# Row sums of four heads in one matmul set, and key and query loads of 64 rows

## The chip, the cores and the metric

The kernel runs on one core of one Trainium2 chip. The metric is the time on the device in microseconds (us). TensorE (PE) does the matmuls, VectorE (DVE) and ScalarE (ACT) the elementwise work, GpSimd (POOL) and SyncE (SP) here mainly issue transfers, which 16 DMA engines carry out.

## The reference, cut to what matters

All is float32, with 2048 tokens, model width 1024 and 32 heads. The change lies in `_A_ref`.

```python
def _A_ref(x, wqkv, wo):                       # S = 2048, D = 1024, H = 32, Dh = 32
    qkv = (x @ wqkv).reshape(B, S, 3, H, Dh).transpose(2, 0, 3, 1, 4)
    q, k, v = qkv[0], qkv[1], qkv[2]
    scores = jnp.einsum("bhqd,bhkd->bhqk", q, k) * (Dh ** -0.5)
    p = _softmax(scores, axis=-1)
    o = jnp.einsum("bhqk,bhkd->bhqd", p, v)
    return o.transpose(0, 2, 1, 3).reshape(B, S, D) @ wo
...
g = _sigmoid((x * gate_w).sum(-1, keepdims=True))
return g * _A_ref(x, A_wqkv, A_wo) + (1 - g) * _B_ref(x, ...)   # B: a router over 64 experts
```

## The kernel before

The program has three stages: projections, router and values; the attention; and the output product with `wo`. In the first, q and k are each split into a high and a low part of lower precision, and `evac` stores the four in DRAM, one array [1024, 2048] for each (`QKD`). Head h owns rows 32h to 32h+31 of each.

The attention works head by head, with a step for every tile of 128 keys: 16 steps a head, 512 in all, done in twos. For two tiles, `scores` puts eight matmuls (four chunks of 512 queries each) into a ring of seven PSUM banks (tile `ring`), and ACT takes the exponentials out of it into P tiles of [128 keys x 2048 queries]. Then PE multiplies the P tiles of the two steps before with the values (`pv`, tile `o`). The key operand holds three blocks of 32 rows (high, high, low) and the query operand three (high, low, high), so that one matmul sums three products; two more rows hold a shift. `load_kq` loads both for head h+1 at step 2 of head h, with six transfers of 32 rows of 8 KB on SP's queue. Even heads use the tiles called z, odd heads K and Q.

The softmax needs for every query the sum of P over all keys. Tile 1 of a head is written into a tile `accd` of its own, and tiles 3, 8 and 12 are added to it by accumulating transfers that POOL issues (`presum`, L1385). DVE adds the other twelve into `ACC[h]`, [128 x 2048] (first L1390, then L1392). `merge`, at step 5 of the next head, adds accd to it (L1395). What is left is a sum over 128 partitions.

Heads 0 to 27 do that in pairs, during the two heads that follow. `fold_even` adds the upper 64 partitions of the even head's ACC to its lower 64 with an accumulating transfer (POOL, L1398). `copy_odd` copies the upper half of the odd head's ACC into the freed upper half of the even one (SP), and `fold_odd` adds the odd one's lower half to that (POOL, L1404). `pair_sums` multiplies with a 0/1 selection matrix `sel` in four matmuls, one for each chunk of queries (L1376, with the tile name prm for the weights), two heads at once; ACT copies the result out of the ring (L1411), and SP stores it. Heads 28 to 30 take their sums one by one with `head_sums`. ACC of heads 4g+2 lies in a tile rb0; the other even heads use acc0, the odd ones acc1.

There are eight P buffers besides accd. A buffer is written again eight tiles later (tile 1 not counted), once PE, DVE or the transfer that reads it is done. The order of each engine's instructions and of each queue is the order in which the program is written: a table `todo` gives for each step what is done after `pv`, and a queue issues strictly in that order. A transfer whose operands are not ready holds up all that come behind it on the same queue.

Of the kernel before, what the change touches and what calls it, by code (L numbers as in the profile page):

```python
# [9 lines left out]
F32 = mybir.dt.float32  # L10
F32R = mybir.dt.float32r
I32 = mybir.dt.int32
AF = mybir.ActivationFunctionType
OP = mybir.AluOpType
AX = mybir.AxisListType

S = 2048
D = 1024
# [3 lines left out]
NT = S // 128  # L22
NQ = S // 512
# [8 lines left out]
def gated_mha_peer_kernel(ctx, tc, xT, wqkv, wv, wo, wq, k12, ug, v, out):  # L32
# [8 lines left out]
    nc = tc.nc  # L41
# [4 lines left out]
    dram = ctx.enter_context(tc.tile_pool(name="dram", bufs=1, space=bass.MemoryType.DRAM))  # L46


    QKD = [[dram.tile([D, S], F32R, name=f"{n}d{part}") for part in "hl"] for n in "qk"]
    SHD = dram.tile([H, 2, S], F32R, name="shd")  # L50
    VD = [dram.tile([S, 512], F32, name=f"vd{i}") for i in range(2)]
    WPD = dram.tile([128, KC, 512], F32, name="wpd")
# [4 lines left out]
    SMD = [dram.tile([4, S], F32, name=f"smd{g}") for g in range(G)]  # L57
# [17 lines left out]
    def dma(dst, src, queue=nc.sync):  # L75
        a, b = (ap.bitcast(F32) if ap.dtype == F32R else ap for ap in (dst, src))
        return queue.dma_start(a, b)
# [16 lines left out]
    def split(hi, lo, src, on=None):  # L94
        nc.scalar.activation(hi, src, AF.Copy)
        (on or nc.vector).tensor_tensor(out=lo, in0=src, in1=hi.bitcast(F32), op=OP.subtract)
# [38 lines left out]
    def hi_of(parts, src):  # L135
        nc.scalar.activation(parts[0], src, AF.Copy)  # L136

    def lo_of(parts, src):
        nc.vector.tensor_tensor(out=parts[1], in0=src, in1=parts[0].bitcast(F32), op=OP.subtract)
# [98 lines left out]
    late = []  # L238

    def run_late():  # L240

        for f, *a in late:
            f(*a)
        late.clear()
# [11 lines left out]
    def evac(which, c, n, src, ps, hold=False):  # L256
        hi, lo = (ev.tile([128, 512], F32R, name=part) for part in ("hi", "lo"))
        hi_of((hi, lo), src)
        run_late()
        if hold:  # L260
            held.append(((hi, lo), src))
        else:
            lo_of((hi, lo), src)
        late.append((squares, ps, src, which, c, n))
        for dst, t in zip(QKD[which], (hi, lo)):
            late.append((dma, dst[128 * c:128 * c + 128, n * 512:(n + 1) * 512], t, nc.gpsimd))

    def load_kq(h, tiles):
        K, Q = tiles
        rows = slice(32 * h, 32 * h + 32)  # L270
        (qh, ql), (kh, kl) = (tuple(t[rows, :] for t in parts) for parts in QKD)
        for tile_, srcs in ((K, (kh, kh, kl)), (Q, (qh, ql, qh))):
            for i, src in enumerate(srcs):
                dma(tile_[32 * i:32 * i + 32, :], src)

    def load_shift(h, tiles):
        dma(tiles[1][96:98, :], SHD[h])
# [532 lines left out]
    def exact_maxima():  # L810
        limit_bits = int(np.float32(SHIFT_LIMIT / SCALE).view(np.int32))
        creg = nc.values_load(cbits.bitcast(I32), min_val=0, max_val=2 ** 31 - 1,
                              skip_runtime_bounds_check_because="a float's bits without its sign")

        banks = [(bank_no[0] + k) % 8 for k in range(7)]

        def bank():
            banks.append(banks.pop(0))
            return ps1.tile([128, 512], F32, name=f"bk{banks[-1]}")

        with tc.If(creg > limit_bits):
            with ExitStack() as st:
                gp = st.enter_context(tc.tile_pool(name="gp", bufs=1))
                with tc.For_i(0, H, 1) as h:
                    kt = gp.tile([96, S], F32R, name="gk")
                    hs, rows = bass.ds(h, 1), bass.ds(h * 32, 32)
                    for i, part in enumerate((0, 0, 1)):
                        dma(kt[32 * i:32 * i + 32, :], QKD[1][part][rows, :])
                    mx = gp.tile([128, NT, 4], F32, name="mx")
                    for t in range(NT):  # L830
                        if t % 8 == 0:
                            qt = gp.tile([96, S // 2], F32R, name="gq")
                            c = slice(t * 128, (t + 8) * 128)
                            for i, part in enumerate((0, 1, 0)):
                                dma(qt[32 * i:32 * i + 32, :], QKD[0][part][rows, c])
                        for n in range(4):
                            ps = bank()
                            nc.tensor.matmul(ps, qt[:, t % 8 * 128:(t % 8 + 1) * 128], kt[:, n * 512:(n + 1) * 512],
                                             start=True, stop=True)
                            nc.vector.tensor_reduce(mx[:, t, n:n + 1], ps, axis=AX.X, op=OP.max)  # L840
                    mr = gp.tile([128, NT], F32, name="mr")
                    nc.vector.tensor_reduce(mr, mx, axis=AX.X, op=OP.max, negate=True)
                    pt = bank()
                    nc.tensor.transpose(pt[:NT, :128], mr, ident)
                    hi = gp.tile([NT, 128], F32R, name="ghi")
                    lo = gp.tile([NT, 128], F32R, name="glo")
                    split(hi, lo, pt[:NT, :128])
                    for r, src in ((0, hi), (1, lo)):
                        dma(SHD[hs, r:r + 1, :].rearrange("a b (t s) -> (a b t) s", t=NT), src)
# [413 lines left out]
    keep = Pool("keep")  # L1263
# [3 lines left out]
    NP = H - 4  # L1267
    ACC = {}

    def new_acc(h):  # L1270
        if h < NP and h % 4 == 2:
            ACC[h] = keep.tile([128, S], F32, name="rb0")
        else:
            ACC[h] = wk.tile([128, S], F32, name=f"acc{h % 2}", bufs=1)

    def raw_wo(kc):
        i, j = divmod((kc - 1) % KC, 2)
# [2 lines left out]
    wk = Pool("wk", bufs=2)  # L1280

    new_acc(0)
    sel = prf
    nc.vector.memset(sel, 0.0)
    for i in range(2):
        nc.vector.memset(sel[64 * i:64 * i + 64, i:i + 1], 1.0)
    vpool = Pool("vpool", bufs=2)
    kq = Pool("kq")
    pools["left"] = Pool("ppl")
# [7 lines left out]
    ring = pss.tile([128, NB, 512], F32, name="ring")  # L1297
# [3 lines left out]
    def ring_banks(n):  # L1301
        i = [(ring_no[0] + k) % NB for k in range(n)]
        ring_no[0] += n
        return i

    def on_ring(ins, *banks):

        for other, theirs in users:
            if ins.ins.engine != other.ins.engine and not theirs & set(banks):
                tc.declare_no_dep(ins.ins, other.ins, reason="different banks of the ring")  # L1310
        users.append((ins, set(banks)))
        del users[:-6 * NB]
# [60 lines left out]
    def rowsum(ps, *srcs, by=ones):  # L1373
        for src in srcs:
            for qc in range(NQ):
                yield nc.tensor.matmul(ps[32 * qc:32 * qc + 32, :], by,  # L1376
                                       src[:, qc * 512:(qc + 1) * 512],
                                       start=(src is srcs[0]), stop=(src is srcs[-1]))
# [15 lines left out]
    def merge(h):  # L1394
        nc.vector.tensor_add(ACC[h], ACC[h], ACCD[h])  # L1395

    def fold_even(h):
        nc.gpsimd.dma_start(ACC[h][:64], ACC[h][64:], accum_op=OP.add)  # L1398

    def copy_odd(h):  # L1400
        dma(ACC[h - 1][64:], ACC[h][64:])

    def fold_odd(h):
        nc.gpsimd.dma_start(ACC[h - 1][64:], ACC.pop(h)[:64], accum_op=OP.add)  # L1404

    def pair_sums(h):
        i, = ring_banks(1)
        for ins in rowsum(ring[:, i, :], ACC.pop(h), by=sel):
            on_ring(ins, i)
        o = wk.tile([128, 512], F32, name="ssb")  # L1410
        on_ring(nc.scalar.activation(o, ring[:, i, :], AF.Copy), i)  # L1411
        g, j = divmod(h, 4)
        for m in range(2):
            dma(SMD[g][j + m:j + m + 1, :].rearrange("o (q s) -> (o q) s", q=NQ), o[m::32, :])

    def head_sums(h):
        i, = ring_banks(1)
# [72 lines left out]
    def at(step, f, *a):  # L1490
        todo.setdefault(step, []).append((f, a))

    for h in range(H):
        base = h * NT
        g, j = divmod(h, 4)
        if h < H - 1:
            at(base + NT, finish, h)
            at(base + NT + 5, merge, h)
            if h >= NP:
                at(base + NT + 8, head_sums, h)  # L1500
            elif h % 2 == 0:
                at(base + NT + 9, fold_even, h)
            else:
                at(base + NT + 8, copy_odd, h)
                at(base + NT + 10, fold_odd, h)
                at(base + 2 * NT + 2, pair_sums, h - 1)
        if j == 3 and g + 1 < G:
            at(base + 2 * NT + 8, load_r, g)
            at(base + 2 * NT + 12, norm_r, g)
        if h >= 1 and h + 1 < H:  # L1510
            at(base + 2, load_head, h + 1)
        if g + 1 < G:
            at(base + 7, load_v, g + 1, j)
    for i, step in enumerate((6, 7, 9, 11)):
        at((H - 1) * NT + step, split_first, i)
    for k in range(2 * KC):
        c = slice(k % 2 * D // 2, (k % 2 + 1) * D // 2)
# [310 lines left out]
```

## Time and profile before

| | |
|---|---|
| median of 3 runs | 1813.65 us (1811.86 to 1818.12) |
| profiled execution | 1815.41 us, of it the span 1813.6 us |
| busy: PE, DVE, ACT, POOL | 99%, 81%, 72%, 14% of the span |
| attention, first scores to last | from about 612 to 1640 us of the span |
| accumulating transfers into accd | 95 of 1 MB, median 8.5 us from issue to landing |
| folds of even heads, issued by POOL | 14 of 512 KB; median 9.3 us (acc) and 13.5 us (rb) |
| folds of odd heads into rb, issued by POOL | 7 of 512 KB, median 7.6 us |

Rows of the timeline read: start in us from the start of the span, duration in us, engine, line, operation, tile written and tiles read, count; in brackets the engine's idle time before it and what ended it. A row of busy times by stretch gives the stretch, its length, the busy time of PE, PEld, DVE, ACT and POOL, each with its number of instructions, the granted clock of TensorE, the busy share of the DMA engines and GB/s. Rows of transfers give the tile written and read, the issuing queue, the count, the size and the median time from issue to landing. q0 is the queue of POOL's transfers, q1 that of SP's. L numbers are lines of the kernel before.

### The profile page before, as it was taken

The page shows a single profiled execution, that of the slowest core. Times are in us where ns is not written, and L with a number is a line of the kernel's source. Part 1 is how long each engine was busy: PE and PEld are TensorE (multiplying, and loading weights), DVE is VectorE, ACT ScalarE, POOL GpSimd, SP SyncE. Part 2 cuts the span into 40 slices and gives each one's busy share as a digit, 9 for nine tenths or more (in the row PEclk, how much of TensorE's full clock was granted, in tenths as well). Part 3 has the DMA queues.
Part 4 walks back from the last instruction along what each step waited for, and adds up shares of the span by engine and source line. Part 5 has one row for each costly group of instructions (what it writes and reads, how often), then busy time and mean ns, then how long its engine had stood idle before and what let it go on. Part 6 is the DMA issues. An engine that isn't in the chain of part 4 may idle for free.

```text
span 1813.6 us, 26222 instructions
## 1 busy us (share of the span) xinstructions
PE 1803.4 (99%) x9959; PEld 1092.1 (60%) x9959; DVE 1473.4 (81%) x1278; ACT 1308.9 (72%) x1708; POOL 253.2 (14%) x381
## 2 busy tenths in 40 slices
PE   9999999999999999999999999999999999999999
PEld 7777777788888644444444444444444444447887
DVE  8866876789967888888898887898889888897874
ACT  6545544532343699999999999999999999994221
POOL 1222222244101100101101011100111010000000
PEclk9999999999999999999999999999999999999999
DMA  7888699560267778998899898899999889878641
GB/s 285 275 280 277 214 298 286 193 225 13 82 232 240 224 162 186 201 196 186 189 213 192 191 206 192 187 208 200 196 191 213 187 188 213 191 160 288 231 157 59
DMA packets 120210, 367.48 MB, mean 203 GB/s; under 512 B 16753, under 2 KB 49793, under 8 KB 96465
## 3 DMA queue, kind: packets, MB, share of 16 engines
q0 software_dynamic: 30192, 159.97, 39.2%
q1 hardware_dynamic: 88584, 203.57, 38.6%
q10 hardware_dynamic: 1304, 2.24, 0.3%
q8 instruction: 79, 1.29, 0.3%
q14 instruction: 51, 0.41, 0.1%
HBM read 171.99 MB, written 72.36 MB: 135 GB/s over the span
## 4 chain that ended last, share of the span: by engine, by line
PE 92%; DMA 4%; ACT 2%; issue 1%; SPq 0%; DVE 0%; ACTq 0%
PE ring L1342 25%; PE o L1363 23%; PE bk L303 15%; PE pa L973 7%; PE bk L973 6%; PE bk L734 5%; DMA accd<-P 4%; PE bk L992 2%; PE bk L291 2%; ACT P L1352 2%; PE bk L342 2%; PE pa L1573 1%; PE ring L1376 1%; PE pa L1580 1%; PE bk L191 0%
## 5 line engine op out<-in xcount | busy, mean ns | idle before, releaser
L1352 ACT ACTIVATE P<-ring 128x512 f32<-128x512 f32 (+2 forms) x1028 | 911.8, 982 | 27.5 <-DMA accd<-P 9.3
L1392 DVE TENSOR_TENSOR acc<-acc,P 128x2048 f32<-128x2048 f32 x250 | 572.9, 2291 | 67.5 <-ACT P L1352 47.8
L1363 PE MATMUL o<-P,V 128*32 128x512 f32 x3840 | 466.3, 600 | 0.0
L1342 PE MATMUL ring<-z,z 98*128 98x512 f32 x1016 | 272.3, 408 | 3.7 <-ACT P L1352 3.7
L1342 PE MATMUL ring<-Q,K 98*128 98x512 f32 x1024 | 273.2, 408 | 0.5 <-ACT P L1352 0.5
L1342 PEld LDWEIGHTS ring<-z,z 98*128 98x128 f32 x1016 | 179.9, 188 | 150.1 <-ACT P L1352 86.3
L1342 PEld LDWEIGHTS ring<-Q,K 98*128 98x128 f32 x1024 | 182.2, 188 | 146.1 <-ACT P L1352 75.7
L1363 PEld LDWEIGHTS o<-P,V 128*32 128x32 f32 x3840 | 99.1, 109 | 223.3 <-issue 215.1
L1385 POOL DMA_DIRECT2D accd<-P x95 | 82.0, 863 | 892.4 <-ACT P L1352 600.2
L1392 DVE TENSOR_TENSOR rb<-rb,P 128x2048 f32<-128x2048 f32 x70 | 160.4, 2292 | 17.4 <-ACT P L1352 11.8
L1390 DVE TENSOR_TENSOR acc<-P,P 128x2048 f32<-128x2048 f32 x25 | 57.3, 2293 | 47.5 <-ACT P L1352 47.5
L303 PE MATMUL bk<-xh,A 128*128 128x512 f32 x336 | 82.8, 396 | 0.0
L303 PE MATMUL bk<-xh,S 128*128 128x512 f32 x336 | 81.3, 393 | 0.0
L303 PE MATMUL bk<-xl,S 128*128 128x512 f32 x336 | 80.3, 391 | 0.0
L136 ACT ACTIVATE hi<-u 128x512 fp32r<-128x512 f32 x42 | 26.6, 632 | 70.1 <-issue 35.4
L303 PEld LDWEIGHTS bk<-xh,A 128*128 128x128 f32 x336 | 62.1, 188 | 23.8 <-issue 5.0
L303 PEld LDWEIGHTS bk<-xl,S 128*128 128x128 f32 x336 | 62.7, 188 | 16.6 <-issue 2.5
L303 PEld LDWEIGHTS bk<-xh,S 128*128 128x128 f32 x336 | 62.4, 188 | 14.5 <-issue 1.7
L973 PE MATMUL pa<-woh,acc 128*128 128x512 f32 x216 | 69.9, 389 | 0.0
L1352 ACT ACTIVATE accd<-ring 128x1024 f32<-128x1024 f32 (+2 forms) x65 | 62.3, 1020 | 0.1
L1395 DVE TENSOR_TENSOR acc<-acc,accd 128x2048 f32<-128x2048 f32 x25 | 57.1, 2286 | 0.3 <-DMA accd<-P 0.3
L521 DVE TENSOR_TENSOR u<-u,bk 128x512 f32<-128x512 f32 x70 | 46.6, 683 | 9.7 <-DMA wpd<-u 5.6
(326 smaller groups left out, 2254.5 us busy)
## 6 DMA issues: line engine op xcount, KB each, us to landing
accd<-P POOLq DMA_DIRECT2D x95, 1024.0 KB, 8.5
wqt<-in_wq SPq DMA_DIRECT2D x64, 512.0 KB
wraw<-in_wqkv SPq DMA_DIRECT2D x28, 512.0 KB
kdh<-hi POOLq DMA_DIRECT2D x32, 256.0 KB, 5.6
kdl<-lo POOLq DMA_DIRECT2D x32, 256.0 KB, 6.5
qdh<-hi POOLq DMA_DIRECT2D x32, 256.0 KB, 6.0
qdl<-lo POOLq DMA_DIRECT2D x32, 256.0 KB, 6.0
z<-kdh SPq DMA_DIRECT2D x32, 256.0 KB
```

The costliest lines, as they stand in the source:

```text
L291: nc.tensor.matmul(b0[w, n], AW[PLAIN[w, ki]][a][:, k, :], X[f"B{ki + 1}{n + 1}"][b][:, k, :], start=first, stop=last)
L303: nc.tensor.matmul(ps, a[i][:, k, :], b[j][:, k, :], start=(k == 0 and i == j == 0), stop=(k == HC - 1 and i == 1))
L521: nc.vector.tensor_tensor(out=out, in0=a, in1=b, op=OP.add)
L734: nc.tensor.matmul(ps, x_part(a, t // 4, kc)[:, tok], b, start=first, stop=last)
L973: nc.tensor.matmul(ps, self.a[a][i][:, k, :], self.b[b][j][k], start=(not first and k == 0 and i == j == 0), stop=(k == HC - 1 and i == 1))
L1342: on_ring(nc.tensor.matmul(ring[:, i, :], K[:98, kt * 128:(kt + 1) * 128], Q[:98, qc * 512:(qc + 1) * 512], start=True, stop=True), i)
L1352: on_ring(nc.scalar.activation(P[h, kt][:, q0 * 512:(q0 + m) * 512].rearrange("p (a m) -> p a m", a=m), ring[:, i:i + m, :], AF.Exp, scale ...
L1363: nc.tensor.matmul(O[h][32 * qc:32 * qc + 32, :], Vt[g][:, kt, 32 * j:32 * j + 32], p[:, qc * 512:(qc + 1) * 512], start=(kt == 0), stop=( ...
L1385: nc.gpsimd.dma_start(ACCD[h], P[h, kt], accum_op=OP.add)
L1390: nc.vector.tensor_add(ACC[h], P[h, 0], P[h, kt])
L1392: nc.vector.tensor_add(ACC[h], ACC[h], P[h, kt])
L1395: nc.vector.tensor_add(ACC[h], ACC[h], ACCD[h])
```

## The change

Three things are changed.

First, the high and low parts of q, and of k, lie in one DRAM array [1024, 2, 2048] each, so that for a row of q or k both parts follow each other. `load_kq` then loads the first block of an operand with one transfer of 32 rows, and the second and third together with one of 64 rows, in which high and low rows alternate. The order of the rows within the product changes alike in both operands, so the sum is the same. Four transfers replace six; the bytes are the same.

Second, every head of 0 to 27 is folded twice. `fold_half` adds the upper 64 partitions to the lower 64 (POOL). `fold_quarter(h, 0)` copies partitions 0 to 31 into a quarter of a group tile `F[g]` (SP), and `fold_quarter(h, 1)` adds partitions 32 to 63 to that quarter (POOL). F lies in rb0; ACC alternates between acc0 and acc1.

Third, `group_sums` takes the sums of four heads with one set of four matmuls, with `sel` now four columns over blocks of 32 rows, one copy by ACT and four stores by SP. Seven sets replace fourteen. A set stands at step 2 of the second head after its group's last.

```diff
-    QKD = [[dram.tile([D, S], F32R, name=f"{n}d{part}") for part in "hl"] for n in "qk"]
+    QKD = [dram.tile([D, 2, S], F32R, name=f"{n}d") for n in "qk"]
+    QK_PARTS = (1, 0), (0, 1)
...
-        for dst, t in zip(QKD[which], (hi, lo)):
-            late.append((dma, dst[128 * c:128 * c + 128, n * 512:(n + 1) * 512], t, nc.gpsimd))
+        for i, t in zip(QK_PARTS[which], (hi, lo)):
+            late.append((dma, QKD[which][128 * c:128 * c + 128, i, n * 512:(n + 1) * 512], t, nc.gpsimd))
...
-        K, Q = tiles
-        rows = slice(32 * h, 32 * h + 32)
-        (qh, ql), (kh, kl) = (tuple(t[rows, :] for t in parts) for parts in QKD)
-        for tile_, srcs in ((K, (kh, kh, kl)), (Q, (qh, ql, qh))):
-            for i, src in enumerate(srcs):
-                dma(tile_[32 * i:32 * i + 32, :], src)
+        for t, which in zip(tiles, (1, 0)):
+            src = QKD[which][32 * h:32 * h + 32]
+            dma(t[:32, :], src[:, QK_PARTS[which][0], :])
+            dma(t[32:96, :], src.rearrange("d a s -> (d a) s"))
...
-        if h < NP and h % 4 == 2:
-            ACC[h] = keep.tile([128, S], F32, name="rb0")
-        else:
-            ACC[h] = wk.tile([128, S], F32, name=f"acc{h % 2}", bufs=1)
+        ACC[h] = wk.tile([128, S], F32, name=f"acc{h % 2}", bufs=1)
...
-    for i in range(2):
-        nc.vector.memset(sel[64 * i:64 * i + 64, i:i + 1], 1.0)
+    for i in range(4):
+        nc.vector.memset(sel[32 * i:32 * i + 32, i:i + 1], 1.0)
...
-    def fold_even(h):
+    F = {}
+
+    def fold_half(h):
         nc.gpsimd.dma_start(ACC[h][:64], ACC[h][64:], accum_op=OP.add)
 
-    def copy_odd(h):
-        dma(ACC[h - 1][64:], ACC[h][64:])
-
-    def fold_odd(h):
-        nc.gpsimd.dma_start(ACC[h - 1][64:], ACC.pop(h)[:64], accum_op=OP.add)
-
-    def pair_sums(h):
+    def fold_quarter(h, i):
+        g, j = divmod(h, 4)
+        if i == 0:
+            if j == 0:
+                F[g] = keep.tile([128, S], F32, name="rb0")
+            dma(F[g][32 * j:32 * j + 32], ACC[h][:32])
+        else:
+            nc.gpsimd.dma_start(F[g][32 * j:32 * j + 32], ACC.pop(h)[32:64], accum_op=OP.add)
+
+    def group_sums(g):
         i, = ring_banks(1)
-        for ins in rowsum(ring[:, i, :], ACC.pop(h), by=sel):
+        for ins in rowsum(ring[:, i, :], F.pop(g), by=sel):
             on_ring(ins, i)
         o = wk.tile([128, 512], F32, name="ssb")
         on_ring(nc.scalar.activation(o, ring[:, i, :], AF.Copy), i)
-        g, j = divmod(h, 4)
-        for m in range(2):
-            dma(SMD[g][j + m:j + m + 1, :].rearrange("o (q s) -> (o q) s", q=NQ), o[m::32, :])
+        for j in range(4):
+            dma(SMD[g][j:j + 1, :].rearrange("o (q s) -> (o q) s", q=NQ), o[j::32, :])
...
-            elif h % 2 == 0:
-                at(base + NT + 9, fold_even, h)
             else:
-                at(base + NT + 8, copy_odd, h)
-                at(base + NT + 10, fold_odd, h)
-                at(base + 2 * NT + 2, pair_sums, h - 1)
+                at(base + NT + 9, fold_half, h)
+                at(base + NT + 10, fold_quarter, h, 0)
+                at(base + NT + 13, fold_quarter, h, 1)
+                if j == 3:
+                    at(base + 2 * NT + 2, group_sums, g)
```

Two places show how the order of the queues changes. The first is POOL's queue in heads 8 and 9, during which the sums of heads 7 and 8 are folded; accd<-P is the add of tile 3, 8 or 12. Before:

```order
L1385 DMA accd<-P_7233 128x2048
L1385 DMA accd<-P_7310 128x2048
L1404 DMA rb_6830<-acc_7046 64x2048
L1385 DMA accd<-P_7361 128x2048
L1385 DMA accd<-P_7444 128x2048
L1385 DMA accd<-P_7527 128x2048
L1398 DMA acc_7254<-acc_7254 64x2048
L1385 DMA accd<-P_7579 128x2048
```

And with the change:

```order
L1381 DMA accd<-P_7213 128x2048
L1381 DMA accd<-P_7289 128x2048
L1396 DMA acc_7026<-acc_7026 64x2048
L1381 DMA accd<-P_7341 128x2048
L1405 DMA rb_6708<-acc_7026 32x2048
L1381 DMA accd<-P_7423 128x2048
L1381 DMA accd<-P_7507 128x2048
L1396 DMA acc_7233<-acc_7233 64x2048
```

Each head has now a half fold behind the add of tile 8, and a quarter add between that of tile 12 and the next head's tile 3.

The second place is SP's queue from the loads of head 8 to the loads of head 9 (od is a head's output, smd the row sums, V values of the next group, wo_raw a piece of `wo` for the last stage). Before:

```order
L77 DMA K_5526<-kdh 32x2048 x2
L77 DMA K_5526<-kdl 32x2048
L77 DMA Q_5527<-qdh 32x2048
L77 DMA Q_5527<-qdl 32x2048
L77 DMA Q_5527<-qdh 32x2048
L77 DMA Q_5527<-shd 2x2048
L77 DMA V<-vd_67 128x4x128
L77 DMA rb_6830<-acc_7046 64x2048
L77 DMA wo_raw_5505<-in_wo 128x1x512
L77 DMA od<-osb 128x2x256
L77 DMA smd_74<-ssb 4x512 x2
L77 DMA z_4909<-kdh 32x2048 x2
```

And with the change:

```order
L78 DMA K_5524<-kd 32x2048
L78 DMA K_5524<-kd 64x2048
L78 DMA Q_5525<-qd 32x2048
L78 DMA Q_5525<-qd 64x2048
L78 DMA Q_5525<-shd 2x2048
L78 DMA V<-vd_65 128x4x128
L78 DMA rb_6708<-acc_7026 32x2048
L78 DMA wo_raw_5501<-in_wo 128x1x512
L78 DMA od<-osb 128x2x256
L78 DMA smd_72<-ssb 4x512 x4
L78 DMA z_4907<-kd 32x2048
L78 DMA z_4907<-kd 64x2048
```

The copy into rb is at the same place in the queue, but of 32 rows, and it now reads what the half fold on POOL's queue writes; such a copy stands in every head's stretch up to head 28, where before it stood in every second one.

More of the change, by code (lines that the diff above doesn't have):

```diff
@@ L827, in exact_maxima @@
                     for i, part in enumerate((0, 0, 1)):
-                        dma(kt[32 * i:32 * i + 32, :], QKD[1][part][rows, :])
+                        dma(kt[32 * i:32 * i + 32, :], QKD[1][rows, QK_PARTS[1][part], :])
                     mx = gp.tile([128, NT, 4], F32, name="mx")
@@ L834, in exact_maxima @@
                             for i, part in enumerate((0, 1, 0)):
-                                dma(qt[32 * i:32 * i + 32, :], QKD[0][part][rows, c])
+                                dma(qt[32 * i:32 * i + 32, :], QKD[0][rows, QK_PARTS[0][part], c])
                         for n in range(4):
```

## The prediction

> **What bounds the kernel now.** The page comes first: which engine is full, and what the chain of waits runs over.
>
> ```profile
> PE 1803.4 (99%) x9959; PEld 1092.1 (60%) x9959; DVE 1473.4 (81%) x1278; ACT 1308.9 (72%) x1708; POOL 253.2 (14%) x381
> PE ring L1342 25%; PE o L1363 23%; PE bk L303 15%; PE pa L973 7%; PE bk L973 6%; PE bk L734 5%; DMA accd<-P 4%; PE bk L992 2%; PE bk L291 2%; ACT P L1352 2%; PE bk L342 2%; PE pa L1573 1%; PE ring L1376 1%; PE pa L1580 1%; PE bk L191 0%
> ```
>
> TensorE carries the chain, and half of it is the attention (L1342, L1363). Two entries there belong to what changes: the row sums (L1376), and 4% in which the chain runs over a transfer that adds a P tile into accd. Next, the busy times by head of the attention, each stretch from one head's first scores to the next's: heads 8, 9, 10, 12, 14, 16, 18 and 28.
>
> ```profile
> 864.56:895.83 31.27, 31.27 (x197) 14.73 (x193) 27.16 (x13) 30.75 (x36) 3.41 (x4) 1.00 0.97 209
> 895.83:927.92 32.09, 32.09 (x205) 14.99 (x201) 27.48 (x15) 31.48 (x39) 2.55 (x3) 1.00 0.91 193
> 927.92:959.80 31.88, 31.70 (x197) 14.57 (x193) 28.37 (x14) 30.37 (x36) 4.01 (x5) 1.00 0.94 204
> 991.95:1024.11 32.16, 31.56 (x196) 14.64 (x192) 28.06 (x14) 30.54 (x36) 3.74 (x5) 1.00 0.94 200
> 1056.26:1090.92 34.66, 33.46 (x197) 14.75 (x193) 29.55 (x14) 30.86 (x37) 4.07 (x5) 0.95 0.93 197
> 1123.05:1155.58 32.53, 31.80 (x197) 14.53 (x193) 28.29 (x14) 30.55 (x37) 3.52 (x5) 1.00 0.92 198
> 1187.72:1220.03 32.31, 31.51 (x196) 14.65 (x192) 28.75 (x14) 30.78 (x37) 4.29 (x5) 1.00 0.94 202
> 1506.10:1538.01 31.91, 31.73 (x196) 14.57 (x193) 27.89 (x14) 30.48 (x37) 3.15 (x4) 1.00 0.94 214
> ```
>
> The columns are length, then PE, PEld, DVE, ACT, POOL, granted clock, DMA share, GB/s. Head 8 is the bare beat: 31.27 us, PE full, ACT 30.75 behind it, DVE with 4.1 to spare, and the DMA engines 97% busy. Head 9 has a row sum in it. The others are longer with no row sum: by 0.61, 0.89, 3.39, 1.26, 1.04 and 0.64. Of head 14's 3.39 some 1.7 (5% of 34.66, its clock being 0.95) is clock. So 6.1 us in all is another wait, shown for head 10 by the chain of waits, PE's timeline, and POOL's with the issue's landing:
>
> ```profile
> 936.90 14.16 DMA accd<-P
> 951.38 1.57 PE L1342 MATMUL ring<-z,z 98*128 98x512 f32 x5
> 953.14 0.98 PE L1342 MATMUL ring<-z,z 98*128 98x512 f32 x3 [0.18 <-ACT P L1352]
> 951.59 0.85 POOL L1385 DMA_DIRECT2D accd<-P  x1 [13.84 <-DMA accd<-P]
> accd<-P POOLq DMA_DIRECT2D x1, 1024.0 KB, 7.1
> ```
>
> Tile 3's add into accd, issued 9.0 us into the head, lands at 951.06, that is 23.1 in; its P buffer is the one that tile 11 needs, so ACT and then PE wait. Head 8 shows no wait: its add (13.0 from 873.58) lands at 22.0. The limit is about 22.3. The next add, issued 0.5 after that landing with nothing before it, takes 7.1.
>
> **The change part by part.**
>
> Row sums. PE's timeline around head 9's:
>
> ```profile
> 895.83 2.11 PE L1342 MATMUL ring<-Q,K 98*128 98x512 f32 x8
> 899.72 2.14 PE L1342 MATMUL ring<-Q,K 98*128 98x512 f32 x8
> 903.52 1.04 PE L1376 MATMUL ring<-rb,prm 128*32 128x512 f32 x8
> 904.50 2.12 PE L1342 MATMUL ring<-Q,K 98*128 98x512 f32 x8
> 908.40 2.11 PE L1342 MATMUL ring<-Q,K 98*128 98x512 f32 x8
> ```
>
> Two tiles take 3.89 or 3.90 (895.83 to 899.72, 904.50 to 908.40); with a row sum 4.78, so 0.87 or 0.88 each. Fourteen become seven: 7 x 0.87 = **-6.1 us**, all on PE. ACT loses seven copies of 0.6, which PE covered. The weights stay 128x32, so each set costs what it did.
>
> Key and query loads. Their rate with 32 rows at a time, and that of 8 KB rows into all 128 partitions (z and t3l at the tail), by the DMA view of 1000 to 1005 and of 1644 to 1648:
>
> ```profile
> DMA packets 219, 1.20 MB, mean 241 GB/s; under 512 B 72, under 2 KB 72, under 8 KB 72
> q1 hardware_dynamic: 219, 1.20, 103.1%
> DMA packets 250, 1.72 MB, mean 430 GB/s; under 512 B 35, under 2 KB 35, under 8 KB 54
> ```
>
> Six loads of 256 KB (1.57 MB) take 6.5 at 241. No row shows a 64-row load; between 241 and 430 I take 430, because it now spreads over more partitions, which is all in which the two rows differ that bears on it: 2.2 for the two small loads, 2.4 for the two large, 4.6 in all, so 1.9 sooner; the other bound is nothing. Two issues fewer on SP lie beside other work. The writes to the reordered rows carry the same pieces of 2 KB, off the path in the projections.
>
> The folds. DMA work per head, at 229 GB/s for adds (1 MB in 4.6, from the row below) and 241 for copies: before, per pair two adds and a copy of 512 KB, 6.8, so 3.4 a head; now an add of 512 KB and of 256 KB and a copy of 256 KB, 4.5. The +1.1 is less than the loads' -1.9.
>
> What it moves is the order. POOL's queue and the folds' landings, DVE's first add, and SP's queue:
>
> ```profile
> q0 software_dynamic: 112, 0.92, 111.0%
> DMA packets 112, 0.92 MB, mean 229 GB/s; under 512 B 0, under 2 KB 0, under 8 KB 0
> 915.29 0.85 POOL L1385 DMA_DIRECT2D accd<-P  x1 [9.72 <-ACT P L1352]
> 915.83 1.15 POOL L1398 DMA_DIRECT2D acc<-acc  x1
> accd<-P POOLq DMA_DIRECT2D x1, 1024.0 KB, 12.2
> acc<-acc POOLq DMA_DIRECT2D x1, 512.0 KB, 13.7
> 928.05 0.89 POOL L1385 DMA_DIRECT2D accd<-P  x1 [11.07 <-PE o L1363]
> accd<-P POOLq DMA_DIRECT2D x1, 1024.0 KB, 6.9
> 934.80 2.29 DVE L1390 TENSOR_TENSOR rb<-P,P 128x2048 f32<-128x2048 f32 x1 [1.19 <-ACT P L1352]
> 933.43 1.45 SPq L77 DMA_DIRECT2D K<-kdh  x2
> 943.00 0.52 SPq L77 DMA_DIRECT2D acc<-acc  x1
> ```
>
> Follow the last head of a group (its sum is folded during the head after it, times from that head's start), to the row sum that PE meets 7.7 into the next (903.52 less 895.83).
> - Tile 3's add lands at 22.0 in head 8. The loads ahead are 1.9 shorter; the odd copy, issued on SP 15.1 in (943.00 less 927.92) beside it, is gone, some 1.0 (half of a 2.2 us copy); the previous head's quarter add now comes before it, +1.1. So 20.2.
> - Tile 8's add: 0.5 and 7.1. The half fold behind it lands 2.0 later (929.5 against 927.5). Tile 12's add, issued 0.5 after tile 8's landing, lands 7.4 after it (6.9 more).
> - The quarter copy waits on SP for the half fold, so it reaches the engines after tile 12's add and lands 1.1 behind it. Behind it on SP stand wo_raw, after some heads rd, and the next head's od, all with time.
> - The quarter add waits on POOL for the copy: 0.5, then 1.1 of transfer and the 2.5 that an add has beside transfer (7.1 less 4.6). Behind it on POOL is only the next tile 3's add, 9.0 into the next head.
>
> Sum: 20.2 + 7.6 + 7.4 + 1.1 + 0.5 + 3.6 = 40.4, which is 9.1 into the next head: PE waits 1.4, say 1.5 with the semaphore, at seven row sums: **+10.5**. ACT has no scores left by then and waits too, and PE has no slack to make it up. Bounds: tile 8's add cannot be issued before its exp, 18.6 in (DVE's start on tile 2, 6.9, and six tiles of 1.95), against 20.7 here, so the wait is at best nothing; with the loads not faster it is 3.4.
>
> The wait in the other heads. Tile 3's landing at about 20 to 21 is inside 22.3, so **-6.1** of waits goes. DVE's first add of a head (6.9 in, 934.80) reuses the buffer that is folded during the head before, and now waits for the quarter add, which lies behind the key loads (issued from 5.5 in): 7 + 4.6 + V's 1.1 + its own 1.1, with landing, some 14 to 15. DVE has 4.1 us a head to spare, and that add's P buffer (tile 0) is next written by tile 9, from 18.6 in; the add takes 2.3, so until 16.2 nothing else waits. Cost nothing; from there on, microsecond for microsecond.
>
> Sum: -6.1 - 6.1 + 10.5 = -1.7. The profiled execution took 1815.41 (span 1813.6 and 1.8 around it), so 1813.7; it lies 1.8 above the median of 1813.65. Against the median: **1812**.
>
> **The rivals.**
>
> *No wait at the row sums.* If the quarter copy shares the engines with tile 12's add instead of queueing, it lands some 4 us sooner and F is ready. For it: between 920 and 925 both queues move at once.
>
> ```profile
> q0 software_dynamic: 113, 0.93, 88.7%
> q1 hardware_dynamic: 230, 0.26, 17.1%
> ```
>
> Against it: from 1000 to 1005 (above) only SP's queue moves, with an add issued at 1000.90 outstanding; 8 KB rows that come second wait. [...] Then -12.2: 1801.5.
>
> *Slower: the chain comes late.* If 64 rows load no faster than 32, tile 3's add lands 1.9 later: at 22 in every head, so the 6.1 stays, and the wait at the row sums is 3.4, 7 x 3.4 = 24. Sum -6.1 + 24 = +18: 1831. It decides from a wait of 1.8 on, where the gains are spent. For it: 97% busy DMA in head 8, so any delay is handed on. Against it: the 430.
>
> *Slower: DVE held by its buffer.* If the quarter add lands after 16.2, by 1 us in the 20 or so heads with the key loads ahead: +20, 1832. [...]
>
> *The row sums cost as before per head*, since weights of four columns run as long as of two: excluded, the matmul set is the same size.
>
> **How the numbers follow.** The forecast 0.44, own range 1805 to 1819 (waits of 0.5 to 2.5); no wait 0.22; late chain 0.19; held DVE 0.09; the rest, unnamed, 0.06, half each way. The range takes in the slower rivals' centres and the no-wait one: 1801 to 1831. 0.3% is 5.4 us, about what a measurement of this kernel tells from no change. Faster by more: the no-wait case, a quarter of the forecast, half the rest: 0.35. Slower: late chain and DVE, a tenth of the forecast, half the rest: 0.35 less what of the late chain stays under 5.4, so 0.32. Same: 0.33.
>
> **What would show it.** In the new profile: row-sum periods 4.78 plus the wait, seven of them; PE idle before the row sum ended by the transfer into rb; the K and Q loads done about 1.9 sooner; tile 3's add under 22 and no chain over accd at tile 11; DVE's first add some 14 in, ended by a transfer, with ACT not waiting. Wrong, if the row sums start 7.7 in without a wait, or ACT waits for P in most heads.

## The result, and the profile after

The change takes 1864.05 us (median of 4, 1859.38 to 1868.68) against 1814.93 beside it (1811.86 to 1818.12): a ratio of 1.0277, 95% interval 1.0249 to 1.0304. The forecast was 1812, with a range of 1801 to 1831. The span of the profiled execution grew from 1813.6 to 1857.5, by 43.9.

The attention accounts for all of that. Here are the busy times of the stretch from the first scores to those of the last two tiles, of the kernel before, then of the change (columns as in the prediction):

```profile
615.15:1632.04 1016.89, 1012.70 (x6233) 471.08 (x6232) 875.16 (x403) 986.21 (x1138) 105.84 (x124) 1.00 0.90 193
```

```profile
614.34:1676.21 1061.87, 1023.07 (x6178) 473.64 (x6177) 874.84 (x405) 981.55 (x1131) 129.28 (x152) 0.98 0.86 191
```

It is 45.0 us longer. TensorE's idle time in it goes from 4.2 to 38.8, which is 34.6 more; its busy time grows by 10.4, although seven row sums (7.3 us busy, by PE's groups of before) are gone. So the work that is left takes 17.7 longer, and the clock column, 0.98, points to the reason.

From the page of the change, the chain that ended last:

```profile
PE 81%; DMA 11%; DVE 3%; ACT 2%; issue 2%; POOL 0%; DVEq 0%; SPq 0%; POOLq 0%; ACTq 0%
PE ring L1338 20%; PE o L1359 18%; PE bk L302 15%; PE pa L972 7%; DMA rb<-acc 6%; PE bk L972 6%; PE bk L733 5%; PE bk L290 2%; PE bk L991 2%; DMA acc<-acc 2%; DMA accd<-P 2%; ACT P L1348 2%; DVE acc L1388 2%; PE bk L341 2%; PE pa L1573 1%
```

The chain now runs over the transfers into rb (the quarter copies and quarter adds) and over the half folds. Two engines wait for them, by the groups of PE and of DVE (busy and mean of one, then the idle time before them and what ended it):

```profile
L1372 PE MATMUL ring<-rb,prm 128*32 128x512 f32 x56 | 12.5, 975 | 28.2 <-DMA rb<-acc 14.0 <-issue 12.3 <-ACT P L1348 1.8
L1386 DVE TENSOR_TENSOR acc<-P,P 128x2048 f32<-128x2048 f32 x32 | 73.3, 2292 | 136.6 <-DMA rb<-acc 116.0 <-ACT P L1348 17.3 <-DMA V<-vd 3.3
```

And one waits for DVE, by the list of waits (total, times, longest):

```profile
ACT P L1348 <- DVE acc L1386: 15.8, 8, 4.6
```

The seven row sums stand still for 28.2 us, 4.0 each. DVE's first add of a head waits 116 us in all for the quarter add, 20 times; it has slack, but eight times the wait reaches ACT, which then cannot write tile 9's P buffer. The lateness is also handed on to the next fold, since the half fold reads what DVE's adds leave:

```profile
POOL acc L1396 <- DVE acc L1391: 9.4, 10, 1.4
```

In periods of two tiles, the distance from one pair's first scores to the next: the seven periods with a row sum and the one behind each are together 40.9 us longer than such a pair with a row sum that waits for nothing (head 9: 10.74 and 5.77 against 3.89, 3.92 and 0.87); the periods at tile 9 add 19.0 in ten heads. The waits at tile 11 (6.1, and 1.7 of clock in head 14) and seven row sums (6.1) are gone. Together +46, close to the 45.0.

Part of those periods is the clock. PE's timeline around head 9's row sum, then busy times there in pieces:

```profile
907.57 1.04 PE L1359 MATMUL o<-accd,V 128*32 128x512 f32 x8
913.50 1.93 PE L1372 MATMUL ring<-rb,prm 128*32 128x512 f32 x8 [4.89 <-DMA rb<-acc]
915.36 3.78 PE L1338 MATMUL ring<-Q,K 98*128 98x512 f32 x8
919.07 2.13 PE L1359 MATMUL o<-P,V 128*32 128x512 f32 x16
```

```profile
908.61:913.50 4.89, 0.00 (x1) 0.03 (x1) 3.50 (x3) 0.78 (x1) 1.69 (x2) 0.92 0.67 126
913.50:915.36 1.86, 1.86 (x8) 0.20 (x9) 1.86 (x1) 0.00 (x0) 0.00 (x0) 0.50 1.02 211
915.36:919.07 3.71, 3.71 (x12) 2.49 (x8) 0.92 (x2) 3.28 (x5) 0.00 (x0) 0.50 0.57 121
919.07:921.13 2.06, 2.06 (x17) 0.45 (x17) 2.06 (x2) 1.26 (x2) 0.00 (x0) 0.89 0.80 215
```

After this wait of 4.89 us TensorE runs at half clock (0.50 in the clock column), so the row sum takes 1.93 in place of 1.04 and the eight score matmuls 3.78 in place of 2.11. The change's clock records hold eight such stretches in the attention, 37.5 us in all; half of that is 18.8, close to the 17.7 of extra busy time. The kernel before had one, of 3.4 us.

Why the quarter add is late stands in the chain of waits, from head 8's start (869.33) to head 9's row sum:

```profile
876.07 2.05 ACT P L1348 x2
878.12 0.29 issue
878.41 12.55 DMA accd<-P
...
891.50 0.53 POOL accd L1381
892.03 9.49 DMA acc<-acc
...
901.58 7.35 DMA rb<-acc
...
909.48 3.78 DMA rb<-acc
913.25 0.25 issue
913.50 1.89 PE ring L1372 x5
```

Tile 3's add lands at 890.96, 21.6 into the head; the half fold, issued behind tile 8's add, lands at 901.52; the quarter copy takes 7.35 for 256 KB; only then does the quarter add start. From 878.41 to 913.25 every step is released by the landing of the one before.

### The profile page after: what moved, and what is told of

Same layout as the page of the kernel before. It is cut to its first block, busy times and chain, and to the rows that moved or that the text cites. A ratio compares the mean times of both kernels' runs of the same rounds, so it can differ in the third digit from the quotient of the medians.

```text
span 1857.5 us, 26086 instructions
## 1 busy us (share of the span) xinstructions
PE 1812.8 (98%) x9903; PEld 1095.0 (59%) x9903; DVE 1473.2 (79%) x1280; ACT 1303.8 (70%) x1701; POOL 276.6 (15%) x409
## 4 chain that ended last, share of the span: by engine, by line
PE 81%; DMA 11%; DVE 3%; ACT 2%; issue 2%; POOL 0%; DVEq 0%; SPq 0%; POOLq 0%; ACTq 0%
PE ring L1338 20%; PE o L1359 18%; PE bk L302 15%; PE pa L972 7%; DMA rb<-acc 6%; PE bk L972 6%; PE bk L733 5%; PE bk L290 2%; PE bk L991 2%; DMA acc<-acc 2%; DMA accd<-P 2%; ACT P L1348 2%; DVE acc L1388 2%; PE bk L341 2%; PE pa L1573 1%
## 5 line engine op out<-in xcount | busy, mean ns | idle before, releaser
L1348 ACT ACTIVATE P<-ring 128x1024 f32<-128x1024 f32 (+2 forms) x1028 | 910.3, 987 | 43.8 <-DVE acc L1386 15.8
L1388 DVE TENSOR_TENSOR acc<-acc,P 128x2048 f32<-128x2048 f32 x320 | 733.3, 2291 | 49.7 <-ACT P L1348 21.0
L1338 PE MATMUL ring<-Q,K 98*128 98x512 f32 x1024 | 281.7, 416 | 5.8 <-ACT P L1348 5.8
L1386 DVE TENSOR_TENSOR acc<-P,P 128x2048 f32<-128x2048 f32 x32 | 73.3, 2292 | 136.6 <-DMA rb<-acc 116.0
L1391 DVE TENSOR_TENSOR acc<-acc,accd 128x2048 f32<-128x2048 f32 x32 | 73.1, 2286 | 0.1
L1405 POOL DMA_DIRECT2D rb<-acc x28 | 21.8, 779 | 249.3 <-DMA rb<-acc 131.2
```

The costliest lines, as they stand in the source:

```text
L1338: on_ring(nc.tensor.matmul(ring[:, i, :], K[:98, kt * 128:(kt + 1) * 128], Q[:98, qc * 512:(qc + 1) * 512], start=True, stop=True), i)
L1348: on_ring(nc.scalar.activation(P[h, kt][:, q0 * 512:(q0 + m) * 512].rearrange("p (a m) -> p a m", a=m), ring[:, i:i + m, :], AF.Exp, scale ...
L1386: nc.vector.tensor_add(ACC[h], P[h, 0], P[h, kt])
L1388: nc.vector.tensor_add(ACC[h], ACC[h], P[h, kt])
```

## The experiments

The theory that came out of this profile and the first runs: the adds, folds and copy of a head make one chain, held together by POOL's queue, that is longer than the beat of 31.27 us, so whatever wait is taken away comes back at another place. Its rivals: that the waits are single faults, each to be mended by itself, and that the DMA engines have too much to move.

### The two halves of the change

The new loads with folds and row sums by pairs as before (`loads_alone`), and the new folds and row sums with six loads of 32 rows as before (`folds_alone`):

```diff
# loads_alone: kept from before
-                at(base + NT + 9, fold_half, h)
-                at(base + NT + 10, fold_quarter, h, 0)
-                at(base + NT + 13, fold_quarter, h, 1)
+            elif h % 2 == 0:
+                at(base + NT + 9, fold_even, h)
...
# folds_alone: kept from before
-            dma(t[:32, :], src[:, QK_PARTS[which][0], :])
-            dma(t[32:96, :], src.rearrange("d a s -> (d a) s"))
+            for i, src in enumerate(srcs):
+                dma(tile_[32 * i:32 * i + 32, :], src)
```

> The kernel before with only the key and query loads of the change (reordered rows, 64-row loads); folds and pair sums as before. Theory: tile 3's add lands about 1.9 us sooner, inside 22.3 us, and the 6 us of waits at tile 11 go: 1809. Rival: the loads do not matter, 1815.

> The change with the six 32-row key and query loads of before; folds and row sums by four as in the change. Theory, late chain: the loads' 1.9 us are missing from the start of the chain and again where the quarter add waits behind the loads, so every wait grows by 2 to 4 us: 7 row sums and some 12 heads, 1890 to 1920. Rival: the loads do not matter, 1864.

Loads alone: 1806.38 us, ratio 0.9965 (0.9952 to 0.9977), a little better than expected. Folds alone: 1874.27, ratio 1.0363 (1.0318 to 1.0409), between the two expectations. So the loads are worth 6 us by themselves and 10 or more within the change; all the harm is in the folds. With the loads alone tile 3's add in head 10 lands sooner, 11.6 us from its issue by the transfer view (14.16 in the prediction's chain), and the chain that ended last has no transfer left:

```profile
accd<-P POOLq DMA_DIRECT2D x1, 1024.0 KB, 11.6
```

```profile
PE 97%; ACT 0%; issue 0%; DVE 0%; ACTq 0%
```

### Taking away one wait at a time

```diff
# sums_later: the row sums four steps later
-                    at(base + 2 * NT + 2, group_sums, g)
+                    at(base + 2 * NT + 6, group_sums, g)
# sums_step9: seven steps later, and what follows them
+                    at(base + 2 * NT + 9, group_sums, g)
-            at(base + 2 * NT + 8, load_r, g)
-            at(base + 2 * NT + 12, norm_r, g)
+            at(base + 2 * NT + 11, load_r, g)
+            at(base + 2 * NT + 15, norm_r, g)
# fold_early: the folds ahead of tile 12's add
-                at(base + NT + 9, fold_half, h)
-                at(base + NT + 10, fold_quarter, h, 0)
-                at(base + NT + 13, fold_quarter, h, 1)
+                at(base + NT + 7, fold_half, h)
+                at(base + NT + 9, fold_quarter, h, 0)
+                at(base + NT + 12, fold_quarter, h, 1)
# third_acc_step9: sums_step9 and a third buffer for ACC
-        ACC[h] = wk.tile([128, S], F32, name=f"acc{h % 2}", bufs=1)
+        ACC[h] = (kq.tile([128, S], F32, name="acc2") if h % 3 == 2 else
+                  wk.tile([128, S], F32, name=f"acc{h % 3}", bufs=1))
```

(The third buffer also needed the small tiles ssb and osb to have one buffer each. With two each the tiles do not fit: 29 KB are left in each partition where 32 are needed. So `third_acc`, the third buffer with the row sums where the change has them, has no measured time.)

> The change with the group's row sums four steps later (step 6 instead of 2 of the second head after the group). Theory, late chain: the change's 49 us are two waits behind one late chain of transfers (half fold, quarter copy, quarter add): TensorE at the seven row sums, 41 us beyond the sets' own cost, and ScalarE at tile 9 of some heads, 19 us, because VectorE's first add has no free buffer; 12 us of gains stand against them. Four steps are 7.8 us, more than the latest quarter add is late (about 5), so the 41 us go and the 19 stay: about 1823. Rival, transfer load: the 7 MB more of adding transfers slow everything, and a wait removed at one place comes back at another: still over 1850.

> The change with the folds issued earlier: half fold at step 7 (before tile 8's add), quarter copy at step 9, quarter add at step 12 before tile 12's add; the same transfers, bytes and row sums. Theory, late chain: the half fold goes out as soon as the merge is done, the quarter add lands before or just after the next head begins, and neither TensorE nor VectorE waits for it; both waits go and the gains stay: 1803. Rival, transfer load: same bytes, so it stays above the kernel before, 1830 or more. Second rival: the fold ahead of tile 8's add delays that and tile 12's add by 2.5 us each and ScalarE waits for P buffers instead: 1815 to 1830.

> The change with the group's row sums at step 9 instead of 2 of the second head after the group (and the reciprocals three steps later). Theory: with the sums at step 6 the quarter add still came late, since the loads of keys and queries no longer wait behind the sums' stores and go ahead of it (landed 16.2 in, sums due at 15.5). At step 9 they are due at 21.4, so no row sum waits and the TensorE clock is not halved after one; VectorE's wait for its buffer stays, 20 to 25 us of waits at tile 9: 1822 to 1828. Rival, transfer load: no better than at step 6, 1838.

> Third buffer for ACC and row sums at step 9. Theory: nothing waits for the folds any more; the attention keeps both gains (7 sets fewer, no wait at tile 11): 1802 plus what the single-buffered small tiles cost in the last stage. Rival, transfer load: waits for accd or P buffers come in their place, over 1815.

All four are faster than the change, and none comes near 1803. Each misses what its theory had expected (1823, 1803, 1822 to 1828 and 1802 in the order above), and all but `sums_later` lie where the rival, the amount of transfers, had put them or above; that rival is tried further down.

| | us | ratio to before | waits that are left |
|---|---|---|---|
| `sums_later` | 1838.83 | 1.0139 (1.0122 to 1.0156) | row sums, tile 9 |
| `fold_early` | 1840.11 | 1.0147 (1.0130 to 1.0164) | tiles 5, 11 and 15 |
| `sums_step9` | 1848.24 | 1.0208 (1.0182 to 1.0233) | tile 9, and one row sum of a single head |
| `third_acc_step9` | 1841.92 | 1.0180 (1.0145 to 1.0216) | tile 11, some at 15 |

With the row sums four steps later, due 15.5 us into the head, the quarter add lands at about 16: in the change the sums' four stores on SP hold the next head's key loads back in these heads (in head 9 stores from 916.11, loads from 918.39, 17.7 in; in head 10, without stores, loads from 946.04, 5.4 in), and now those go ahead of it. So this run's row sums wait too (10.4 us in all), and its expectation was wrong. Seven steps later no row sum of a group stands still (PE's groups), though that of one single head near the end does, for 7.5 us. DVE waits nearly as long as in the change, and ACT longer (waits):

```profile
L1372 PE MATMUL ring<-rb,prm 128*32 128x512 f32 x56 | 8.2, 659 | 0.0
```

```profile
DVE acc L1386 <- DMA rb<-acc: 103.1, 17, 11.2
ACT P L1348 <- DVE acc L1386: 25.9, 9, 5.5
```

With the folds early, the quarter add stands on POOL ahead of tile 12's add and waits there for its copy, so that accd is late instead (waits):

```profile
POOL rb L1405 <- DMA rb<-acc: 223.9, 23, 15.6
ACT P L1348 <- DMA accd<-P: 37.8, 30, 4.1
```

With a third buffer neither the row sums nor DVE have anything to wait for, and what is left is the chain itself. POOL's timeline there:

```profile
890.15 0.86 POOL L1382 DMA_DIRECT2D accd<-P  x1 [12.11 <-DMA accd<-P]
890.69 1.18 POOL L1397 DMA_DIRECT2D acc<-acc  x1
897.91 0.89 POOL L1382 DMA_DIRECT2D accd<-P  x1 [6.05 <-DMA accd<-P]
908.66 0.78 POOL L1406 DMA_DIRECT2D rb<-acc  x1 [9.86 <-PE ring L1339]
909.18 1.17 POOL L1382 DMA_DIRECT2D accd<-P  x1
923.49 0.85 POOL L1382 DMA_DIRECT2D accd<-P  x1 [13.14 <-DMA accd<-P]
924.03 1.17 POOL L1397 DMA_DIRECT2D acc<-acc  x1
931.20 0.89 POOL L1382 DMA_DIRECT2D accd<-P  x1 [6.01 <-DMA accd<-P]
941.48 0.78 POOL L1406 DMA_DIRECT2D rb<-acc  x1 [9.39 <-PE ring L1339]
```

And its waits:

```profile
ACT P L1349 <- DMA accd<-P: 36.0, 21, 3.8
```

The rows are tile 8's add, the half fold, tile 12's add, the quarter add, the next head's tile 3's add, and again. Tile 8's add comes round after 33.34 us (890.15 to 923.49), the quarter add after 32.82 (908.66 to 941.48). The run's chain of waits shows the links between the two half folds:

```profile
890.69 9.47 DMA acc<-acc
...
900.21 7.90 DMA rb<-acc
...
909.18 13.78 DMA accd<-P
...
924.03 10.34 DMA acc<-acc
```

The half fold releases the copy, the copy the quarter add, behind which tile 3's add leaves, and its landing releases tile 8's add and the next half fold: a closed loop, here longer than the beat of 31.27 by 1.5 to 2.1. Single rounds differ (30.5 to 35.5 between quarter adds); the mean of the 27 rounds is 33.0, and 31.6 in `no_copy` below. What does not fit returns at tile 11, where the kernel before had waited, and at some tiles 15. (The release that the list names at the quarter add, PE's, had long been there; its place in time fits the copy, issued at 900.21 and landed at 908.11 by that run's chain of waits.)

### Making the loop shorter

```diff
# no_copy
-            dma(F[g][32 * j:32 * j + 32], ACC[h][:32])
+                nc.vector.memset(F[g], 0.0)
# no_add12
-    SUMS = {h: (1, 3, 8, 12) for h in range(H)} | {0: (4, 8, 12), H - 1: (2, 4, 6, 11)}
+    SUMS = {h: (1, 3, 8) for h in range(H)} | {0: (4, 8, 12), H - 1: (2, 4, 6, 11)}
# no_add12_step4: no_add12, and
-                    at(base + 2 * NT + 2, group_sums, g)
+                    at(base + 2 * NT + 4, group_sums, g)
# loads_no_add12: loads_alone, with SUMS as in no_add12
```

> The change without the quarter copy: F is set to zero by DVE once in a group instead (some 1 to 2 us, DVE has 4.1 to spare in a head), and the quarter add adds onto that, so the row sums lack the partial sums of one half of the partitions. All other adds stay. Closed-loop theory: the quarter add no longer waits on POOL for the copy, so it is issued right behind tile 12's add and not 7.3 us into the next head, lands 6 to 8 in, and neither the row sums nor DVE's first add nor tile 3's add wait for long: 1803 to 1812. Rival, it is the amount of transfers that fills the beat: the copy is 0.25 MB of some 6.5 MB in a head, 1.1 us of 31.3, in 28 heads, so it takes 1835 or more.

> The change, with tile 12 of every head added by VectorE instead of by a transfer (1 MB of adding transfers less per head, one VectorE add of 2.29 us more; the row sums stay the same). Theory: the quarter copy no longer queues behind tile 12's add and lands 4 to 5 us sooner, so row sums and VectorE's first add find their data: 1803 to 1810. Rival: VectorE, at 27.5 + 2.3 of 31.3 us a head, cannot take it up and P buffers come free late: 1815 to 1840.

> The change without the transfer add of tile 12 (DVE adds that tile), and the row sums two periods (two tiles each) later, due 11.6 us into the head in place of 7.7. Closed-loop theory: without tile 12's add the quarter add lands 6.9 to 10.8 us into the next head, so only the three row sums that still waited (6.5, 5.3 and 5.9 us periods against 4.8, some 3.4 to 5 us in all) have anything to gain: 1805 less 3 to 4, so 1801 to 1803. Rival, a later row sum moves the sums' stores and the next loads so that the quarter add lands later again, as it did when only the row sums were moved: the waits stay and it takes 1805 or more.

> The kernel before with the new key and query loads alone (row sums by pairs, folds as before), and without the transfer add of tile 12 (DVE adds that tile, 2.3 us more of its 4.1 us to spare in a head). Closed-loop theory: the new loads alone have already ended every wait at tile 11, so there is nothing left for the missing add to end: 1805 to 1808, as the loads alone (1806.4). Rival, the DMA engines' load as such slows the kernel and 1 MB less per head is worth something by itself: 1802 or less; the gain of the change without tile 12's add over the loads alone would then be due to that and not to the fewer row sums.

| | us | ratio to before |
|---|---|---|
| `no_copy` | 1806.18 | 0.9962 (0.9948 to 0.9976) |
| `no_add12` | 1805.22 | 0.9961 (0.9945 to 0.9976) |
| `no_add12_step4` | 1799.96 | 0.9928 (0.9914 to 0.9941) |
| `loads_no_add12` | 1805.24 | 0.9956 (0.9943 to 0.9969) |

`no_copy` is a trial of the timing alone: it leaves half of the partial sums out of the row sums. (Setting F to zero costs 1.6 us seven times, by DVE's busy time of 1484.5 against the change's 1473.2.) Without the copy some 55 us go (49.1 slower than the kernel before becomes 6.2 faster), for 256 KB less of transfer in a head; the three adds into accd, the half fold and the quarter add stay. Busy times of the attention, the group of the row sums, and DVE's wait:

```profile
615.32:1620.95 1005.63, 1002.20 (x6177) 469.44 (x6175) 886.18 (x412) 982.09 (x1131) 128.50 (x151) 1.00 0.88 194
```

```profile
L1372 PE MATMUL ring<-rb,prm 128*32 128x512 f32 x56 | 7.4, 598 | 3.2 <-issue 2.1 <-DMA rb<-acc 1.1
```

```profile
DVE acc L1386 <- DMA rb<-acc: 55.4, 21, 4.1
```

The DMA engines are as busy as in the change (0.88 against 0.86) and the clock is whole. So it is not the amount of transfers but the copy's place as a link: POOL issues the quarter add 2.4 us into the next head at the latest, where the change does so 4.4 to 9.7 in. Taking tile 12's add out instead, behind which the copy queues, does the same with the copy in place, and DVE has the room for that tile. With the row sums two steps later (`no_add12_step4`) their last waits go as well, by the busy times of its attention:

```profile
616.31:1617.63 1001.32, 1001.11 (x6177) 469.88 (x6176) 942.41 (x435) 981.60 (x1131) 102.42 (x122) 1.00 0.77 172
```

PE is idle for 0.2 us of 1001. This version beats both kernels: 0.9928 of the one before. The control shows that tile 12's add alone is worth nothing where no wait is left: 1805.24, as with the loads alone. From there to 1799.96, both on one chip, are 5.3 us; seven row sums at 0.87 would be 6.1.

## Why the prediction was wrong, point by point

**Row sums, -6.1.** About right, though only to be seen once nothing waits: 5.3 between `loads_no_add12` and `no_add12_step4`. A set costs what it did: 592 ns a matmul in `no_add12_step4`, as before.

**Loads, 6.5 to 4.6 us.** Right in sign. The transfer view of the change from 787 to 789, within the key and query loads of one head (issued by SP from 784.35 to 786.57):

```profile
DMA packets 106, 0.66 MB, mean 328 GB/s; under 512 B 26, under 2 KB 26, under 8 KB 26
```

328 GB/s in these 2 us, between the two ends (241 and 430); over 785 to 790, which takes in more of the 32-row and 64-row loads and V, it is 261. The rows do not tell the two kinds of load apart, and that the rate grows with the partitions a load spreads over was the author's estimate from the rows at 241 and 430; no run tried it by itself. With the loads alone tile 3's add in head 10 took 11.6 in place of 14.16, 2.6 sooner where 1.9 was computed; in head 8, which had not waited, it landed 20.3 into the head in place of 22.0. The late chain's reason, loads no faster than before, fell with it.

**The wait at tile 11, -6.1.** Right: gone in the change and in the loads alone, which are 0.35% faster (0.23 to 0.48).

**The copy queues behind tile 12's add.** Right, and the rival with no wait at the row sums falls. The transfer view of the change from 938.5 to 941.5, with the copy issued at 938.40 by SP and tile 12's add moving:

```profile
q0 software_dynamic: 80, 0.66, 105.3%
```

Nothing on SP's queue in 3 us, while 80 rows of 8 KB moved on POOL's: here the copy's 8 KB rows, which came second, waited for those of the add, which came first.

**The chain, 40.4.** This is the step that failed first. In head 8, from its start at 869.33, tile 3's add landed at 21.6 (computed 20.2), the half fold at 32.2 (29.8), the copy at 39.6 (36.3), the quarter add at 43.9 (40.4), so the row sum waited 4.9 and not 1.5; the seven stood for 28.2 us, not 10.5. (In the 1.5, the 0.1 for the semaphore was an estimate; the change's chain has 0.25 from the landing at 913.25 to the row sum.) In the terms of the sum, 20.2 + 7.6 + 7.4 + 1.1 + 0.5 + 3.6 became 21.6 + 7.8 + 8.6 + 1.6 + 0.5 + 3.8. Two of them make most of the difference. Tile 3's add went out 9.1 in as forecast, but took 12.6, beside the key loads and a quarter add that was itself still on its way (issued 7.0 in, landed 14.1) and had been counted as 1.1 us in front. Tile 12's add took 8.6 for 7.4; the half fold beside it landed 2.8 behind tile 8's add and not 2.0. The prediction walked the chain once, from a head's start to the next head's row sum. It never asked whether a head's chain fits in a head's beat: closed, it takes about 33 us (`third_acc_step9`) against 31.27, and where it does not fit, the lateness stays or is paid with a wait.

**DVE's first add, cost nothing.** Wrong, by 19.0. The threshold held: the ten heads whose first add began after 16.2 (16.7 to 20.7 in) are the ten with a longer period at tile 9, and in all others it began by 15.5. What was wrong is that 14 to 15 was taken for every head. In those ten the quarter add was issued 7.3 to 9.6 in and landed 16.5 to 20.5 in, beside the key loads and the next tile 3's add. Of all 28 quarter adds, those of a group's last heads took 3.7 or 3.8 us, of its first 5.3 to 7.7, of its second and third 7.2 to 11.3; the third is as slow as the second, and what makes this order no run shows. As a rival this had 0.09, as a size 20 (1 us in some 20 heads, which was the author's estimate; the trace has 19.0 in ten heads); it came beside the late chain, not in its place.

**The clock.** Not in the sum. The forecast costed a wait at its length; about 18 us, over a third of the loss, are the extra time of work at half clock after the waits. Head 14 of before (3.39 us longer, 1.7 of it clock) was read and not carried over to the waits that were forecast.

So the late chain was the right rival, with a wrong reason and a price too low. Its 18 holds a wait of 24 at the row sums (measured 28.2), but neither the half clock behind them (12.7, the rest of the 40.9) nor DVE's 19.0, which includes its own share of half clock; and it kept the waits at tile 11, which went.

## What to carry to other kernels

Where transfers depend on each other through one issuing queue, add up the chain around the loop, from one landing to the same landing a beat later, and compare it with the beat. Here it was longer, 33.0 against 31.27: moving the work about only moved the wait (1838.83 to 1848.24 in four runs), until a link went (1799.96 to 1806.18). What such a link cost here was its wait for a landing and not its bytes (the copy of 256 KB: some 55 us in all). Cost a TensorE wait of some microseconds at more than its length: here each of the change's seven waits of 3.2 us or more in the attention was followed by half clock.

## What the runs showed of the hardware

In the attention of the kernel before and of the change, each of the seven idle stretches of TensorE of 3.2 to 5.6 us was followed by half clock, beginning 1.7 to 5.4 us after the wait's start, and of the three of 1.0 to 1.8 us one was. By the clock records the stretches at half clock are 3.4 us long (six) or 6.8 (three), and one of the nine had no single wait of 1 us in front of it. That the wait causes it was not tried by itself; it is what stands together in these traces. Over the whole profiled execution the granted clock is 1.00 in the five kernels `loads_alone`, `no_copy` and the three without tile 12's add (TensorE's idle time in the attention is 0.2 us in `loads_alone` and `no_add12_step4` and 3.4 in `no_copy`), and 0.986 to 0.996 in the five others that were run beside the change. How the DMA engines share between two queues beyond the rows shown stays open.
